# An exp queue's costs in an ordering simulation: two constants and the settings of an attention kernel's instruction order

## The chip, the cores and the metric

One core of a Trainium2 chip. The metric is the device time of one execution in microseconds; the median of three runs stands for a kernel.

## The reference

Attention with normalised queries and keys, 32 heads, 2048 positions, 20 columns per head, bf16 inputs:

```
qn = q / (sqrt(sum(q*q)) + 1e-6);  kn = k / (sqrt(sum(k*k)) + 1e-6)
logits = einsum('bhqd,bhkd->bhqk', qn, kn) * t[head]
out = einsum('bhqk,bhkd->bhqd', softmax(logits), v)
```

With 20 columns per head the matrix products are thin; the 32 x 2048 x 2048 exponentials are the bulk of the work.

## The kernel before

**Units.** Four heads form a group (eight groups), and 512 query positions of a group form a superblock (32 of them, `sb`). A superblock's scores fall into 64 units: one head, 128 key positions on the partitions, 512 queries along the columns; 2048 units in all. TensorE makes the scores of a unit with one matmul over a strip of 32 rows (line 793); four heads can run side by side on the four strips.

**Two ways to an exponential.** ScalarE takes two units at once: a *wave*, two matmuls into one of two slots of the PSUM tensor psA and one exp over 128 x 1024 into pA (line 995). VectorE takes single units: scores into a bank of psD, then one instruction that multiplies, adds and converts to int16, so that the bits read as float16 approximate an exponential (dI, line 361). GpSimd (POOL) adds two constants to these bits, as 64-bit integers of four values each, giving dS1 and dS2 (line 374); one POOL instruction can cover up to four units. Their weighted sum is the approximation.

**The second product.** A PV matmul (line 815) multiplies exponentials with v and a column of ones and accumulates in one bank of psD; the four heads of a round run side by side on four column strips. A unit from ScalarE needs one PV matmul (source pA), one from VectorE four (dI with vaug, dI with vhalf, dS1 and dS2 with vaug). At the end of a superblock VectorE transposes the bank out (accT, line 386), takes the reciprocal of the ones' column and multiplies (lines 400 and 401), and the output goes out by DMA.

**Preparation.** For each next group q, k and v are loaded on SP's queue, squares are summed (a transpose on SP, then small matmuls, line 749), the norms are worked out on VectorE, and q and k go through DMA transposes (line 446) to qT and kT. Early in the kernel, where TensorE has little to do, it runs matmuls on zeros (line 612), which the program calls heating.

**What sets the order.** `make_plan` simulates the five engines in steps of 5 ns while the program is built. Each operation has a `cost` (how long its engine is taken) and a `lat` (when its result is there); the engines choose by rules what to do next, and the order that comes out is each engine's instruction stream, with semaphore waits for the dependences. Which units go to ScalarE and which to VectorE also comes out of it: whoever is free first takes the next. An exp enters with these two values:

```
a = Op("ACT", "exp", ..., ACT0 + n_u * QW / 1200.0, ACT1 + n_u * QW / 1200.0)
```

For a wave n_u * QW is 1024. A psA slot is free for the next wave when the exp's `lat` is over, and the rules ask how far away that is: for instance, no PV round begins within PVHOLD of it. The rules' settings (`RULES`) can differ for every ten waves: character i of ORDER picks an entry of CHOICES, 23 sets of changed settings, for waves 10 i to 10 i + 9. On the chip only the order and the waits remain; each engine goes through its stream as fast as its waits allow.

The program holds a second plan, in which ScalarE makes all exponentials; a flag read from t picks one of the two at run time. In the runs here the first is used.

Of the kernel before, what the change touches and what calls it, by code (L numbers as in the profile page):

```python
# [30 lines left out]
CHOICES = ({}, dict(JOINB=1), dict(DURG=2), dict(RUN=2), dict(PVHOLD=(0, 0)), dict(PVHOLD=(.4, .4)), dict(DFIRST=0), dict(PVHOLD=(.33, .33)),  # L31
           dict(PRIO=1.1), dict(PMIN=3), dict(PGAP=.15), dict(JOINB=9), dict(TWICED=1), dict(PVHOLD=(.15, .15)), dict(POOL_MAX=2), dict(DURG=0),
           dict(PVHOLD=(.2, .3)), dict(PVHOLD=(.3, .2)), dict(NEEDW=1), dict(PSLACK=.1), dict(JOINB=1, DURG=2), dict(PVHOLD=(.2, .2), DURG=2), dict(BACK=12))
ORDER = "0305080i2k7lj3700hj2e0me07cj08i7a1i0j01g2bjb5j5080i00g017fl67g60"

PARTS = ((0, 4), (4, 16))
NH = 4
# [31 lines left out]
PV_MAX = 100  # L69
POOL0 = .162  # L70
POOLL = .05
ACT0 = .05
LOAD0 = 2.75
TRL = 2.25
TRK = 1.2
PLAG = .03
LOCKL = 0.12
ACT1 = .33
PEL = .17
POOL1 = .0009  # L80
POOL2 = .00166
# [75 lines left out]
def bass_standalone__qk_norm__prompt_kernel(  # L157
# [15 lines left out]
    with ExitStack() as es:  # L173
# [295 lines left out]
        def make_plan(share):  # L469
# [476 lines left out]
            def step_pe0():  # L946
# [25 lines left out]
                if parts and slot_free and not any(x[3] in held for x in pending_pv):  # L972
# [4 lines left out]
                    if keys_ready(us):  # L977
# [6 lines left out]
                        if cur > 0 and not cur_free() and in_use() < S.HEATQ:  # L984
# [11 lines left out]
                               [("psA", slot)], [("pA", pslot, i) for i in range(WAVES[slot])],  # L996
                               ACT0 + n_u * QW / 1200.0, ACT1 + n_u * QW / 1200.0)
                        P.link(a)
# [294 lines left out]
            while True:  # L1293
                if share and len(waves) // STRETCH > stretch:
                    stretch = len(waves) // STRETCH
                    vars(S).update(RULES, **CHOICES[int(ORDER[stretch:stretch + 1] or "0", 36)])
                moved = True
# [190 lines left out]
```

## Time and profile before

| | before |
|---|---|
| median of three runs | 596.71 us (596.52 to 599.08) |
| the profiled execution's own time | 596.55 us |
| its span, first to last instruction | 594.4 us |
| busy: TensorE, VectorE, ScalarE, POOL | 582.6, 574.4, 582.3, 498.2 us |
| mean granted TensorE clock | 0.998 |
| exps on ScalarE | 630 |

Busy time is the union of an engine's records. A record of ScalarE or VectorE can overlap the next on its engine, and matmuls are pipelined, so a busy engine is not necessarily one that could do no more: the distance between the ends of records tells more than their lengths. "PE" is TensorE's matmul, "PEld" its weight load, "SPq" the issue of a DMA. In the tables a row has the source line, engine, operation, and result<-sources.

### The profile page before, as it was taken

To read this page: it belongs to the slowest core of one execution; us is meant where nothing else is said; L and a number is where in the kernel's file an instruction comes from. 1 tells how busy PE (TensorE), PEld (TensorE's weight loads), DVE (VectorE), ACT (ScalarE), POOL (GpSimd) and SP (SyncE) were. 2 spreads that over 40 slices of the span, in tenths; PEclk is the share of its full clock that TensorE was granted. 3 is DMA by queue.
4 is the path that set the end of the run, shared out by engine and by line. 5 is a ranking of instruction groups with operands and counts; after the bars stand their busy time and mean duration, and the time that the engine had idled before them with its cause. 6 is when DMAs were issued, how large, how long until landed. Compare 5 with 4: busy or idle time off the path is not lost.

```text
span 594.4 us, 16322 instructions
## 1 busy us (share of the span) xinstructions
PE 582.6 (98%) x6741; PEld 154.0 (26%) x6741; DVE 574.4 (97%) x1012; ACT 582.3 (98%) x638; POOL 498.2 (84%) x947
## 2 busy tenths in 40 slices
PE   8999999999999999999999999999999999999996
PEld 4332222322222222222222222222222222222221
DVE  6899999999999999999999999999999999999995
ACT  6999999999999999999999999999999999999995
POOL 2498898888988879879898889978899798999995
PEclk9999999999999999999999999999999999999999
DMA  8701405105042051410534022340405204010000
GB/s 117 107 2 26 92 2 67 25 1 116 3 45 46 2 116 8 62 23 3 113 22 72 2 52 67 24 68 2 99 2 52 57 1 73 2 24 8 1 13 10
DMA packets 132143, 24.18 MB, mean 41 GB/s; under 512 B 121312, under 2 KB 132064, under 8 KB 132064
## 3 DMA queue, kind: packets, MB, share of 16 engines
q1 hardware_dynamic: 131264, 22.96, 24.4%
q8 instruction: 54, 0.88, 0.7%
q14 instruction: 25, 0.20, 0.1%
q10 hardware_dynamic: 800, 0.12, 0.1%
HBM read 7.87 MB, written 2.62 MB: 18 GB/s over the span
## 4 chain that ended last, share of the span: by engine, by line
ACT 83%; PE 13%; SPq 1%; POOL 1%; DMA 1%; DVE 1%; issue 0%
ACT pA L995 83%; PE psD L815 7%; PE psA L793 5%; POOL dS L374 1%; PE psD L612 1%; SPq L437 1%; DMA vaug<-in_v_dram 1%; PE psD L793 1%; DVE dI L361 0%; SPq L427 0%; DVE accT L386 0%; DVE ost L401 0%; SPq L577 0%; PE psD L658 0%; DVE rec L400 0%
## 5 line engine op out<-in xcount | busy, mean ns | idle before, releaser
L995 ACT ACTIVATE pA<-psA 128x1024 f16<-128x1024 f32 (+1 forms) x630 | 578.1, 1254 | 1.8 <-PE psD L793 0.9
L374 POOL INT64_ADD dS<-dI x931 | 491.8, 544 | 77.6 <-DVE dI L361 14.6
L361 DVE TENSOR_SCALAR dI<-psD 128x512 int16<-128x512 f32 (+1 forms) x764 | 488.1, 695 | 8.1 <-PE psD L793 5.6
L793 PE MATMUL psA<-qT,kT 32*128 32x512 bf16 x1260 | 245.2, 384 | 2.2 <-ACT pA L995 0.8
L793 PE MATMUL psD<-qT,kT 32*128 32x512 bf16 x793 | 240.7, 383 | 0.1
L815 PE MATMUL psD<-dS,vaug 128*22 128x512 f16 x1576 | 196.3, 383 | 1.4 <-POOL dS L374 1.4
L815 PE MATMUL psD<-pA,vaug 128*22 128x512 f16 (+1 forms) x1260 | 172.5, 383 | 1.1 <-DMA vaug<-in_v_dram 0.9
L815 PE MATMUL psD<-dI,vaug 128*22 128x512 f16 x788 | 130.6, 382 | 0.0
L815 PE MATMUL psD<-dI,vhalf 128*22 128x512 f16 x788 | 128.6, 383 | 0.0
L793 PEld LDWEIGHTS psA<-qT,kT 32*128 32x128 bf16 x1260 | 59.1, 91 | 251.7 <-ACT pA L995 246.2
L793 PEld LDWEIGHTS psD<-qT,kT 32*128 32x128 bf16 x793 | 56.3, 91 | 7.4 <-issue 3.6
L815 PEld LDWEIGHTS psD<-dS,vaug 128*22 128x22 bf16 x1576 | 42.1, 89 | 57.4 <-issue 30.7
L815 PEld LDWEIGHTS psD<-pA,vaug 128*22 128x22 bf16 x1260 | 36.7, 89 | 49.3 <-issue 45.4
L815 PEld LDWEIGHTS psD<-dI,vhalf 128*22 128x22 bf16 x788 | 28.2, 89 | 30.9 <-issue 21.7
L815 PEld LDWEIGHTS psD<-dI,vaug 128*22 128x22 bf16 x788 | 29.0, 89 | 23.1 <-issue 17.6
L386 DVE STREAM_TRANSPOSE accT<-psD 128x512 f32<-128x512 f32 x32 | 22.6, 705 | 2.7 <-PE psD L815 2.7
L401 DVE TENSOR_TENSOR ost<-accT,rec 128x320 bf16<-128x320 f32 x32 | 16.4, 512 | 0.1
L264 DVE TENSOR_TENSOR sqs<-qk 128x1280 bf16<-128x1280 bf16 x14 | 11.9, 849 | 0.0
L749 PE MATMUL psD<-ind,sqT 128*128 128x128 bf16 x140 | 11.6, 221 | 0.0
L749 PEld LDWEIGHTS psD<-ind,sqT 128*128 128x128 bf16 x140 | 7.9, 98 | 5.2 <-issue 5.0
L612 PE MATMUL psD<-zt 128*128 128x128 bf16 x106 | 9.2, 221 | 0.0
L322 DVE RECIPROCAL rn<-rsa 128x128 f32<-128x128 f32 (+2 forms) x10 | 7.8, 780 | 0.1
(59 smaller groups left out, 81.5 us busy)
## 6 DMA issues: line engine op xcount, KB each, us to landing
vaug<-in_v_dram SPq DMA_DIRECT2D x32, 80.0 KB, 4.2
qk<-in_k_dram SPq DMA_DIRECT2D x7, 320.0 KB, 4.4
out_dram<-ost SPq DMA_DIRECT2D x28, 80.0 KB, 1.9
qk<-in_q_dram SPq DMA_DIRECT2D x6, 320.0 KB, 4.1
qk<-in_q_dram SPq DMA_DIRECT2D x4, 80.0 KB, 2.8
out_dram<-ost SPq DMA_DIRECT2D x7, 40.0 KB, 2.0
qk<-in_k_dram SPq DMA_DIRECT2D x1, 240.0 KB, 3.6
qk<-in_q_dram SPq DMA_DIRECT2D x1, 240.0 KB, 4.3
```

The lines of the kernel that those rows point to most:

```text
L264: ops.append(dve("sq", w_, R2, lambda e, o=sq, x=x3: e.tensor_tensor(o, x, x, ALU.mult), [("qk", b, a, i) for i in parts] + [("qkx", b, i) ...
L322: add("inv", lambda e: e.reciprocal(rn_, ra), [K("ra")], RN[a0:a1], R1, n * 5 * R1)
L361: lambda e: e.tensor_scalar(dst, psD[:, pb * QW:(pb + n) * QW], 1024.0 * LOG2E, 15360.0 - 1024.0 * LOG2K + SHIFTS[0], ALU.mult, ALU.add),
L374: lambda e: e.int64_add(o.bitcast(U64), x.bitcast(U64), add), rd, wr)
L386: return dve("drain", QW, R1, lambda e: e.transpose(accT[:, 16 * b:16 * b + 16, :].rearrange("p b d -> p (b d)"), psO_(sb)), [("psD", OB(s ...
L401: dve("omul", 320 * n, R1, lambda e: e.tensor_tensor(dst, num, rcb, ALU.mult), at + ar, [("ost", hg % 2, g) for g in range(g0, g1)]),
L437: ops.append(dma("ldv", lambda e, d=d_, s=s_: e.dma_start(d, s), [], [("v", b, hh)], 1.4, 4.0))
L612: return lambda e: e.matmul(bank, zt[:, 0:128], zt[:, 0:n], start=False, stop=False, skip_group_check=True)
L749: mms = [lambda e, g=g, j=j: e.matmul(dst, sqT[:, (5 * g + j) * 128:(5 * g + j + 1) * 128], ind[:, j, 96 - 32 * g:224 - 32 * g], start=g + ...
L793: return lambda e: e.matmul(dst, lhsT, rhs, tile_position=(32 * hh, 0))
L815: return lambda e: e.matmul(dst, lhsT, rhs, start=first, stop=last, skip_group_check=True, tile_position=(0, 32 * hh))
L995: a = Op("ACT", "exp", lambda e, s=src, d=dst: e.activation(d, s, ACT.Exp), [("psA", slot)], [("pA", pslot, i) for i in range(WAVES[slot]) ...
```

## The change

Two costs of an exp in the simulation, and the string of settings:

```
-ORDER = "0305080i2k7lj3700hj2e0me07cj08i7a1i0j01g2bjb5j5080i00g017fl67g60"
+ORDER = "01i6e8h7238em08g57h5hi2i0gi1j2i0lgea8aa50a567i6538abh965h237050"
...
-ACT0 = .05
+ACT0 = .0633
...
-ACT1 = .33
+ACT1 = .17
```

For a wave the simulated distance between two exps on ScalarE goes from 0.903 to 0.917 us, and the time from an exp's start to its result from 1.183 to 1.023 us. No instruction's form changes. The order does, on all engines. In the streams of the two built programs, first plan:

| | before | after |
|---|---|---|
| exps (waves) | 630 | 628 |
| units for VectorE | 788 | 792 |
| dI instructions (of them double) | 764 (24) | 768 (24) |
| int64 adds on POOL | 931 | 935 |
| PV matmuls | 4412 | 4424 |
| heating matmuls | 106 | 123 |
| PV phases of one, two, three rounds | 141, 434, 29 | 153, 387, 55 |
| PV matmuls behind the last psA pair | 28 | 40 |

A phase is a run of PV matmuls between two other operations of TensorE.

## The prediction

> **What bounds the kernel now.** I read the page's busy shares first, then the chain that ended last, then the windows of the middle, to see whether the engine named by the chain ever rests.
>
> ```profile
> span 594.4 us, 16322 instructions
> PE 582.6 (98%) x6741; PEld 154.0 (26%) x6741; DVE 574.4 (97%) x1012; ACT 582.3 (98%) x638; POOL 498.2 (84%) x947
> ACT 83%; PE 13%; SPq 1%; POOL 1%; DMA 1%; DVE 1%; issue 0%
> ```
>
> Three engines look full, so shares decide nothing. The chain says ScalarE, and its pieces in order of time (start, length, what) say where:
>
> ```profile
> 25.59 6.11 POOL dS L374 x14
> 31.75 0.40 PE psD L815 x4
> 32.47 0.80 PE psD L815 x12
> 33.62 491.45 ACT pA L995 x536
> ...
> 587.09 1.69 PE psD L815 x28
> 588.80 0.73 DVE accT L386
> ```
>
> One unbroken piece of 536 exps takes 491.45 us: 0.9169 us for each wave of 1024 columns. Behind 525 us the chain hops between engines, but the windows show ScalarE busy to the last hundredth there too (columns: length, then busy time and count of PE, PEld, DVE, ACT, POOL, then clock, DMA share, GB/s):
>
> ```profile
> 40.00:140.00 100.00, 99.83 (x1149) 25.15 (x1146) 99.06 (x169) 100.00 (x111) 84.69 (x161) 1.00 0.25 42
> ...
> 540.00:580.00 40.00, 39.89 (x484) 10.32 (x480) 38.97 (x68) 40.00 (x45) 38.02 (x73) 1.00 0.04 8
> sum 540.00, PE 538.32 PEld 136.55 DVE 534.87 ACT 540.00 POOL 470.28; mean PE 89.72 PEld 22.76 DVE 89.14 ACT 90.00 POOL 78.38
> ```
>
> ACT 540.00 of 540.00: from 40 us on the kernel is a queue of exps at 0.917 us. So I ask of the change: how many exps, can they start to be dense sooner, does anything let the queue run dry, and what follows the last one.
>
> **How much lateness the queue forgives.** An exp's record is longer when it queues behind the one before it:
>
> ```profile
> L995 ACT ACTIVATE pA<-psA x630: 1018/1262/1346, 8.6 to 587.1; 128x1024 f16<-128x1024 f32 x157, 128x1024 bf16<-128x1024 f32 x1
> ```
>
> (minimum/median/maximum in ns.) 1.02 us is an exp that found the engine free, 1.346 one whose scores came as early as two psA slots allow. TensorE may thus be up to 1.346 - 1.018 = 0.33 us late with a wave before ScalarE idles. This stretch of TensorE shows how it gets late:
>
> ```profile
> 134.62 0.39 PE L793 MATMUL psA<-qT,kT 32*128 32x512 bf16 x2
> ...
> 135.69 0.39 PE L793 MATMUL psA<-qT,kT 32*128 32x512 bf16 x2
> 135.70 0.60 PE L793 MATMUL psD<-qT,kT 32*128 32x512 bf16 x2
> 136.23 0.60 PE L815 MATMUL psD<-dS,vaug 128*22 128x512 f16 x6
> ...
> 136.77 0.39 PE L793 MATMUL psA<-qT,kT 32*128 32x512 bf16 x2
> 136.78 0.39 PE L793 MATMUL psD<-qT,kT 32*128 32x512 bf16 x1
> 137.09 0.60 PE L815 MATMUL psD<-pA,vaug 128*22 128x512 f16 x5
> ...
> 137.64 0.39 PE L793 MATMUL psA<-qT,kT 32*128 32x512 bf16 x2
> ```
>
> From one psA pair to the next: 1.07 us with three rounds of four PV matmuls behind it, 1.08 with two score passes and two rounds (both scores of a strip in one phase), 0.87 with one pass and two rounds. The first two are long against 0.917, by 0.16 each; the ordinary one wins 0.046 back. The exps of that place:
>
> ```profile
> L995 ACT ACTIVATE pA<-psA x3: 1023/1027/1187, 136.1 to 138.1; 128x1024 f16<-128x1024 f32 x3
> ```
>
> Two long stretches on end, 0.33 in sum, use up all the allowance (1.023) and still cost nothing. That is the scale by which I judge the new order.
>
> **The change, part by part.** All counts are of the two built programs' instruction orders. The two constants and the settings act only through the order, so its effects are these.
>
> *Fewer waves.* 630 exps become 628; four units of work go to VectorE instead (792 for 788). ScalarE: 2 x 0.917 = 1.83 us less on the path. A rule that would make this term vanish: by the Trainium skill's page Perfetto Trace Analysis (section Optimizing Scalar/DVE Operations) an instruction of ScalarE on PSUM costs about 51 ns beside its elements, an estimated 0.904 us for such a wave, which is the old setting's pitch; the trace's 0.917 over 536 waves disagrees and decides.
>
> *More on VectorE.* Four more dI instructions (768 for 764, 24 of them double in both). The first eight show their pitch:
>
> ```profile
> 22.90 4.93 DVE L361 TENSOR_SCALAR dI<-psD 128x512 int16<-128x512 f32 x8 [0.88 <-PE psD L793]
> L361 DVE TENSOR_SCALAR dI<-psD 128x512 int16<-128x512 f32 x740 | 461.1, 678 | 7.7 <-PE psD L793 5.5 <-PE psA L793 0.3
> ```
>
> (4.93 - 0.68)/7 = 0.61 us, so +2.4 us. Its window also shrinks: by the 1.83, by the start term below, and by another 1.83 because the last unit for VectorE now stands in the fifth wave from the end instead of the third: some 5 us. Against 7.3 us in all stand 5.1 us of visible idle in the windows (540 - 534.87), and bubbles inside busy time: 461.1/740 = 0.623 where 0.61 is the pitch, about 10 us over 740. It fits, with little left. I put it at 0 and keep 4 us as the upper end. POOL gets four more int64 instructions (935 for 931) and has 70 us idle in the windows. On SP nothing is added; in one head group q's transpose goes ahead of k's, in others four output transfers swap with a transpose. Each group has some 74 us (594/8), so I take 0; without that cover a landing is at stake:
>
> ```profile
> kT<-kpad SPq DMA_TRANSPOSE x8, 4.3
> ```
>
> *TensorE's order.* The mean work between two waves, from passes, rounds and switches as above, is the same, 0.878 us in both orders. But it is spread less evenly: long stretches (over 0.95) go from 54 to 87 behind the 28th wave, PV phases of three rounds from 29 to 55. I added up lateness along both orders (stretch minus 0.917, never below 0). Before: highest 0.34 and 0.34, at the place shown and at one near 470 us; the trace has exps of 1.02 us at exactly these. After: highest 0.37 in one cluster around wave 484, then 0.33 and 0.30. Against 0.33 that is an idle of some 0.05 us. I allow 0.2 for this and for waits on POOL that fall badly; lower end 0, since a queue that is never dry cannot gain.
>
> *The start.* Here the queue does run dry:
>
> ```profile
> 22.99 4.75 ACT L995 ACTIVATE pA<-psA 128x1024 f16<-128x1024 f32 x5
> 25.59 1.89 POOL L374 INT64_ADD dS<-dI  x5 [7.38 <-DVE dI L361]
> 27.90 0.10 PEld L815 LDWEIGHTS psD<-dS,vaug 128*22 128x22 bf16 x4 [1.73 <-POOL dS L374]
> 28.66 5.98 ACT L995 ACTIVATE pA<-psA 128x1024 f16<-128x1024 f32 x6 [0.92 <-PE psD L793]
> ```
>
> The exps end at 27.74, the next at 28.66 + 1.02 = 29.68: 1.94 for 0.917, 1.03 lost. The sixth of that piece ends at 34.64 (28.66 + 5.98) where 29.68 + 5 x 0.917 = 34.27 would do: 0.37 lost. Cause: the first int64 add runs at 25.59, though its input was there near 23.6 (22.90 + 0.68); it waits for something that no row names; I take it to be the cost of POOL's first instruction of this kind. The first PV on dS waits for the sixth POOL instruction. In the new order the same PV stands one wave later (+0.917 us), and waits for the fifth, since the first ones take two units at once. At 1.89/5 = 0.38 each that is 25.59 + 5 x 0.38 = 27.5, against an arrival of TensorE near 27.2: 0.3 us late instead of 1.43, inside the allowance. So 1.40 us go, if POOL starts at 25.59 again. Ends: 0 to 1.40; I take 1.40, because both facts (a wave later, one POOL instruction fewer) point the same way. Seventeen more heating matmuls (123 for 106) lie ahead of this, where TensorE waits for ScalarE; uncovered, each would cost
>
> ```profile
> 20.13 0.68 PE L612 MATMUL psD<-zt 128*128 128x128 bf16 x9
> ```
>
> (0.68 - 0.23)/8 = 0.06 us, 1 us in all.
>
> *The tail.* Behind the last psA pair stood 28 PV matmuls, now 40.
>
> ```profile
> 583.36 4.96 ACT L995 ACTIVATE pA<-psA 128x1024 f16<-128x1024 f32 x5
> 586.70 0.39 PE L793 MATMUL psA<-qT,kT 32*128 32x512 bf16 x2
> 587.02 0.40 PE L815 MATMUL psD<-pA,vaug 128*22 128x512 f16 x4
> ```
>
> ScalarE ends at 588.32, TensorE 0.47 later (588.79). A round is (1.69 - 0.40)/6 = 0.215, so three more are 0.65. Before, the last pair was 0.16 late behind a three-round stretch; after, only two-round ones stand ahead of it, and it should come about 0.24 earlier against the exps. Net +0.41; ends 0 and +0.65.
>
> **The sum.** -1.83 - 1.40 + 0.41 + 0.2 = -2.6. The profiled execution took 596.55 us (594.4 of span, 2.15 around it), so 593.9; the median of the runs is 596.71, 0.16 above, so I say 594.1 for the median. A measurement of this kernel can tell about 0.5%, 3.0 us, from no change: 593.7 is the border of faster, and the forecast lies just inside "same".
>
> **The rivals.**
>
> *The start's stall stays* or moves to the next PV that needs POOL: -1.83 + 0.41 = -1.4, 595.3. For it: POOL's late start isn't touched by the change. Against: the later PV.
>
> *VectorE runs out of slack.* ScalarE then waits for scores whose bank VectorE hasn't freed. Against: the bubbles above. Price: up to the 4 us that I couldn't cover, 595 to 598.
>
> *The long stretches bite* (the other side). The new costs let TensorE be late by design; if the allowance in practice is below 0.16 us, because waits on POOL already use half of it, each long stretch empties the queue by 0.16. The 33 more alone: 5.3 us, 599.4; all 87: 14 us, 608. I take 601. Against it speaks the place at 136 us; for it that the wait table has 136 waits for POOL:
>
> ```profile
> PEld psD L815 <- POOL dS L374: 38.5, 136, 1.7
> ```
>
> (38.5 us in sum, the longest 1.7.) It decides from a lateness of 0.33 on.
>
> *ScalarE isn't the limit*: its own pitch is smaller, and TensorE paces it. Then two waves fewer bring nothing, and start and tail leave -1.0: 595.7. The mechanism would show as exps of 1.02 us throughout; the median is 1262. This is where the 51 ns of the Trainium skill (Perfetto Trace Analysis) would lead.
>
> *More than summed*: the tail hides its rounds and nothing is late: -1.83 - 1.40 = -3.2, 593.5.
>
> **How the numbers follow.** Forecast 0.53 (its own range 593.4 to 594.9), start stays 0.14, VectorE 0.13, long stretches 0.14, ScalarE not the limit 0.03, more than summed 0.03. Faster by over 0.5% (under 593.7): about 0.4 of the forecast's own case, and the last: 0.25. Slower by over 0.5% (over 599.7): most of the long stretches, a little of VectorE: 0.14. Same: 0.61. For 8 in 10 I leave out the long stretches and trifles below: 593.1 to 598.6.
>
> **What would show it.** Right: 628 exps; one ScalarE piece of the chain at 0.917 per wave; the last exp ending near 585.1 (588.32 - 3.23) and the last transpose of accT starting near 586.0; TensorE's wait for dS near 27.5 us under 0.5. The start is wrong if ScalarE still has a gap of 0.9 near 28 us; the queue step is wrong if the windows from 40 us on show ACT under 100.00, and the partner named in ScalarE's waits (a dI bank or a dS) tells VectorE from the long stretches. The forecast as a whole is wrong above 595.

## The result: 594.4 us for 596.5

The changed kernel takes 594.38 us (median of 9 runs, 593.94 to 594.82), the kernel before 596.52 (median of 9); the ratio is 0.9961, 95% interval 0.9949 to 0.9974: 2.1 us or 0.4% less, clear of noise but inside "same" (under 0.5%), and 0.3 from the forecast of 594.1. As a change it is -2.1 where -2.6 was forecast: the median of the kernel before is 596.52 in this group of runs, 0.2 below the 596.71 that the forecast started from. The profiled execution took 594.49 us. Its page:

```profile
span 592.7 us, 16383 instructions
PE 581.3 (98%) x6768; PEld 160.2 (27%) x6768; DVE 574.6 (97%) x1016; ACT 580.4 (98%) x636; POOL 500.9 (84%) x951
ACT 87%; PE 10%; DVE 2%; POOL 1%; issue 0%
L995 ACT ACTIVATE pA<-psA 128x1024 f16<-128x1024 f32 (+1 forms) x628 | 576.2, 1201 | 0.5 <-PE psD L793 0.2
```

The shares say nothing new. The count does (628), and so does the mean of an exp: 1201 ns where it was 1254. The line before was

```profile
L995 ACT ACTIVATE pA<-psA 128x1024 f16<-128x1024 f32 (+1 forms) x630 | 578.1, 1254 | 1.8 <-PE psD L793 0.9
```

The exps queue less long, TensorE is later with them. The chain in order of time:

```profile
25.35 3.87 POOL dS L374 x8
...
51.27 517.24 ACT pA L995 x564
...
584.58 2.30 PE psD L815 x40
586.90 0.73 DVE accT L386
```

ScalarE's piece has 517.24/564 = 0.9171 us per wave, against 0.9169 before: still dense, with 0.2 us of idle time hidden in it (564 x 0.9167 = 517.02). The start, from ScalarE's, POOL's and TensorE's rows in order of time:

```profile
9.47 20.34 ACT L995 ACTIVATE pA<-psA 128x1024 bf16<-128x1024 f32 x22 [0.19 <-PE psA L793]
25.35 2.69 POOL L374 INT64_ADD dS<-dI  x6 [6.93 <-DVE dI L361]
27.72 0.10 PEld L815 LDWEIGHTS psD<-dS,vaug 128*22 128x22 bf16 x4 [0.42 <-POOL dS L374]
29.27 0.10 PEld L815 LDWEIGHTS psD<-pA,vaug 128*22 128x22 bf16 x3 [0.59 <-POOL dS L374]
30.03 8.36 ACT L995 ACTIVATE pA<-psA 128x1024 f16<-128x1024 f32 x9 [0.22 <-PE psD L793]
```

The first PV on dS runs at 27.72 instead of 27.90 although POOL starts almost as late (25.35 for 25.59); one wave later in the order, it costs ScalarE nothing. A later PV round that waits for POOL (29.27, for 0.59 us) does: the 22nd exp ends at 9.47 + 20.34 = 29.81, and the next one at 30.03 + 1.02 = 31.05, 1.24 behind for 0.917. So 0.33 us are lost, where the kernel before lost 1.40 in this part.

Added up from the ends of all exp records (distances above 0.917), up to the last transpose of accT, in us:

| | before | after | difference |
|---|---|---|---|
| waves x 0.917 | 630 | 628 | -1.83 |
| first exp's end, with the wait for v behind the first waves | 10.32 | 10.54 | +0.22 |
| ScalarE idle, 20 to 40 us | 1.39 | 0.33 | -1.06 |
| ScalarE idle behind 40 us | 0.00 | 0.32 | +0.32 |
| last exp's end to the last transpose of accT | 0.49 | 0.93 | +0.44 |
| sum | | | -1.91 |
| start of that transpose, measured | 588.80 | 586.90 | -1.90 |

The second row isn't the order's: over the fourteen profiles of this study it lies between 10.0 and 10.7, as the loads land. The third row is one execution's, too: before_exp6 and before_qk33 (below), whose first 40 us are those of the kernel before, lost 1.10 and 1.02 there, and after_exp6 and after_dve8 0.22 and 0.24. So the start's gain is 0.7 to 1.2 us.

The table ends at the last transpose of accT, and two stretches lie outside it. From that transpose to the end of the span it is 5.58 us before and 5.84 after (5.5 to 6.4 over the fourteen profiles). And an execution's time exceeds its span by 2.17 us before and 1.75 after: by 2.1 to 2.3 in the runs of the kernel before, by 1.7 to 1.9 in those of the changed one. For the two profiled executions -1.90 + 0.26 - 0.42 = -2.06, from 596.55 to 594.49. What makes the 0.42 no run here shows.

### The profile page after: what moved, and what is told of

It reads as the page before. It is cut to its first block, busy times and chain, and to the rows that moved or that the text cites. A ratio compares the mean times of both kernels' runs of the same rounds, so it can differ in the third digit from the quotient of the medians.

```text
span 592.7 us, 16383 instructions
## 1 busy us (share of the span) xinstructions
PE 581.3 (98%) x6768; PEld 160.2 (27%) x6768; DVE 574.6 (97%) x1016; ACT 580.4 (98%) x636; POOL 500.9 (84%) x951
## 4 chain that ended last, share of the span: by engine, by line
ACT 87%; PE 10%; DVE 2%; POOL 1%; issue 0%
ACT pA L995 87%; PE psD L815 4%; PE psA L793 3%; PE psA L616 1%; PE psD L612 1%; POOL dS L374 1%; DVE dI L361 0%; PE psD L793 0%; PE psD L749 0%; DVE ssum L294 0%; DVE accT L386 0%; DVE sqs L291 0%; DVE kpad L338 0%; PE psD L616 0%; DVE ost L401 0%
## 5 line engine op out<-in xcount | busy, mean ns | idle before, releaser
L995 ACT ACTIVATE pA<-psA 128x1024 f16<-128x1024 f32 (+1 forms) x628 | 576.2, 1201 | 0.5 <-PE psD L793 0.2
L793 PE MATMUL psD<-qT,kT 32*128 32x512 bf16 x795 | 237.6, 383 | 0.1
L815 PE MATMUL psD<-dS,vaug 128*22 128x512 f16 x1584 | 201.2, 383 | 0.1
L815 PE MATMUL psD<-pA,vaug 128*22 128x512 f16 (+1 forms) x1256 | 181.1, 383 | 0.3 <-POOL dS L374 0.3
L815 PE MATMUL psD<-dI,vaug 128*22 128x512 f16 x792 | 133.9, 383 | 0.0
L815 PE MATMUL psD<-dI,vhalf 128*22 128x512 f16 x792 | 131.4, 383 | 0.0
L815 PEld LDWEIGHTS psD<-pA,vaug 128*22 128x22 bf16 x1256 | 39.6, 89 | 49.6 <-issue 41.2
L815 PEld LDWEIGHTS psD<-dI,vhalf 128*22 128x22 bf16 x792 | 29.7, 89 | 27.4 <-issue 20.0
L612 PEld LDWEIGHTS psD<-zt 128*128 128x128 bf16 x123 | 7.0, 98 | 4.9 <-issue 4.9
```

Of the source, the lines that this page charges most:

```text
L612: return lambda e: e.matmul(bank, zt[:, 0:128], zt[:, 0:n], start=False, stop=False, skip_group_check=True)
L793: return lambda e: e.matmul(dst, lhsT, rhs, tile_position=(32 * hh, 0))
L815: return lambda e: e.matmul(dst, lhsT, rhs, start=first, stop=last, skip_group_check=True, tile_position=(0, 32 * hh))
L995: a = Op("ACT", "exp", lambda e, s=src, d=dst: e.activation(d, s, ACT.Exp), [("psA", slot)], [("pA", pslot, i) for i in range(WAVES[slot]) ...
```

## The experiments

Each prediction of a kernel stands on the sum that the forecast used: waves, idle time at the start, lateness over 0.33 us, tail. The medians are compared with the kernel before in the same group of runs.

**One half of the change each.** The costs without the settings, the settings without the costs, and both without the new latency:

```
costs_only:  ACT0 = .0633, ACT1 = .17, ORDER as before
order_only:  ACT0 = .05,   ACT1 = .33, ORDER as after
pitch_only:  ACT0 = .0633, ACT1 = .33, ORDER as after
```

> The two new costs with the old settings. The order that comes out has 632 waves (before 630, after 628), 81 long stretches of TensorE, 52 PV matmuls behind the last psA pair, and the first PV on dS at the old place behind six POOL instructions. Theory (ScalarE is a dense queue; time is waves x 0.917 + losses at the start + tail): +1.83 for the waves, the start's 1.4 us stay, six more rounds in the tail +1.1; 599.4 against 596.5, 598.8 to 600. Rival (long stretches empty the queue, 0.16 each): 27 more of them add 4.3 us, 603.7.

> The new settings with the two old costs. The order has 632 waves, 86 long stretches, 88 PV matmuls behind the last psA pair, and the first PV on dS one wave later behind five POOL instructions. Theory: +1.83 for the waves, -1.1 to -1.4 at the start, +3.0 for fifteen more rounds in the tail, some 0.3 of lateness over 0.33: 600.1 against 596.5, 599.4 to 600.8. Rival (long stretches): +5.1 on top, 605.

> The new settings and the new distance of 0.917 with the old latency of 1.183. The order has 628 waves like the changed kernel, 68 PV matmuls behind the last psA pair and 107 long stretches. Theory: the waves' gain is the distance's alone; +1.5 for seven more rounds in the tail than the changed kernel has, +1.1 of lateness over 0.33 by adding up the order: 597.0 against 594.4 for the changed kernel and 596.4 before. Rival (the latency is what counts): 599 or more.

Measured: costs_only 599.21 for 596.35 (ratio 1.0045, 1.0031 to 1.0058); order_only 600.81 for 596.35 (1.0072, 1.0059 to 1.0086); pitch_only 597.72 for 596.47 (1.0016, 1.0003 to 1.0028). Expected were 599.4, 600.1 and 597.0: the first was met, the second came out at the upper end of its range, the third 0.7 above. All three are slower than the kernel before, so here the gain needs both halves. With the old latency alone (pitch_only) the order has the same 628 waves as the changed kernel and takes 3.3 us more. The ends of their chains (costs_only, order_only, pitch_only):

```profile
588.13 2.94 PE psD L815 x51
591.10 0.73 DVE accT L386
```

```profile
588.49 4.89 PE psD L815 x88
593.40 0.73 DVE accT L386
```

```profile
586.24 3.81 PE psD L815 x68
590.07 0.73 DVE accT L386
```

With the last exps ending at 589.41, 589.88 and 587.47 the tails are 1.7, 3.5 and 2.6 us for 52, 88 and 68 PV matmuls; the kernel before has 0.5 for 28. Their long stretches (81, 86, 107) cost 0.2, 0.7 and 2.0 us of idle time behind 40 us, where adding up lateness had given some 0.3 for the second and 1.1 for the third. So a long stretch has no fixed price, and for these two the sum was too kind by about a factor of two. The rival of 0.16 each is out (603.7, 605). The 3.3 us of pitch_only over the changed kernel are 1.7 in the tail and 1.7 of idle time behind 40 us.

**ScalarE longer by six exps.** The added exp reads the same scores and writes to a tile of its own:

```
+ again = [id(o) for o in plans[0][0].order["ACT"] if o.name == "exp"][90::90][:6]
+ again = {x: again_scr for x in again}
...
+ elif id(o) in again:
+     o.emit(eng, d=again[id(o)][:, :])
+     o.emit(eng).then_inc(sems[e], 1)
```

> The kernel before with six of its exps done twice, the first time into a tile of its own (waves 90, 180, ... 540); the order is untouched. Theory (ScalarE is the limit from the first waves to the end): 6 x 0.917 = +5.5 us, 602.0 against 596.5. Rival (ScalarE is paced by TensorE): 0 to 1.

> The changed kernel with six exps done twice in the same way. Theory (still ScalarE): +5.5 less what little idle time there is behind the first 40 us, 599.9 against 594.4, 599.4 at least. Rival (VectorE or TensorE has become the limit in stretches): clearly less than 5.5, say 2 to 4, since an exp more would fall into waiting time.

Measured: 601.67 for 596.66 (1.0073, 1.0052 to 1.0095) and 599.98 (1.0041, 1.0017 to 1.0066, against the kernel before; the changed kernel stands at 0.9961). Two pieces of the second one's chain:

```profile
92.98 82.50 ACT pA L996 x90
176.40 82.55 ACT pA L996 x90
```

92.98 + 82.50 = 175.48, the next piece begins at 176.40: the exp between them costs its whole 0.92. Within a piece 82.50/90 = 0.9167. In the changed kernel ScalarE is still the limit, with 0.05 of idle time in some pieces.

**VectorE and TensorE longer.** In the changed kernel eight dI instructions are done twice; in the kernel before 33 waves have their score matmuls done twice:

```
+ again = [... order["DVE"] if o.name == "P1" and o.cost < .7][85::85][:8]      (after_dve8)
+ again = set(... order["PE"] if o.name == "QKA"][40::17][:33])                  (before_qk33)
+ for mm in o.info * (1 + (id(o) in again)):
```

> The changed kernel with eight of VectorE's dI instructions done twice, the first time into a tile of its own, 85 apart; the order is untouched. Theory (VectorE's bubbles can close): at most 8 x (0.61 - 0.33) = 2.2 us where TensorE is late by more than the allowance, more likely 0 to 1: 594.4 to 595.4. Rival (VectorE has no slack left): 8 x 0.61 = 4.9 us, 599.3.

> The kernel before with the score matmuls of 33 waves done twice (every 17th from wave 40), 0.21 us more for TensorE at each; 80 long stretches instead of 54. Theory (lateness up to 0.33 us is forgiven): adding lateness up along the order leaves 0.4 us over the allowance, 596.9 against 596.5. Rival (a long stretch costs ScalarE 0.16): +5.3, 601.8.

after_dve8: 596.45 (0.9993 against the kernel before, 0.9971 to 1.0016), 2.0 us over the changed kernel: the upper end of what the theory allowed (8 x (0.61 - 0.33) = 2.2), not the 4.9 of a VectorE that is full. Its exp records give 2.35 us of idle time behind 40 us for 0.32: 0.25 more for each added instruction on average, of the 0.61 that it takes, and between 0.14 and 0.33 in the 8 us behind each. TensorE's waits for a dI bank (sum, number, longest), in the changed kernel and in this one:

```profile
PEld psD L793 <- DVE dI L361: 4.8, 22, 0.4
PEld psD L794 <- DVE dI L362: 8.7, 33, 0.5
```

Eleven waits more: VectorE's delay reaches ScalarE through TensorE's queue, and on average 0.36 us of it are forgiven, about the 0.33 of the theory. "More likely 0 to 1" was too hopeful.

before_qk33: 597.37 for 596.66 (1.0003, 0.9975 to 1.0031); the runs of this group scatter more than the effect. The traced execution took 596.53, one of the shorter ones, so the trace tells what the added matmuls cost in it and not what made others longer. Its exps (minimum/median/maximum) and ScalarE's piece of the chain:

```profile
L995 ACT ACTIVATE pA<-psA x630: 1017/1162/1322, 9.2 to 587.1; 128x1024 f16<-128x1024 f32 x157, 128x1024 bf16<-128x1024 f32 x1
33.22 491.81 ACT pA L995 x536
```

491.81 for 536 waves, 0.36 more than before (491.45), the median exp 1162 for 1262: 33 delays of 0.21 us are eaten by the queue almost whole, as added up (0.4). The +5.3 of the rival is out by the times as well.

**POOL's first add.** One more int64 add, on zeros, early in POOL's stream:

```
+ o = Op("POOL", "warm", lambda e: e.int64_add(wscr[...], zt[...], 0), ["zt", ...], ["wscr"], 0.01, 0.05)
```

> The kernel before, with one more int64 add on POOL, on zeros into a tile of its own, ahead of POOL's last early memsets; every other instruction stands as it was. Theory: what delays POOL's first real add until 25.6 us is the cost of its first instruction of that kind; paid some 2 us earlier, the adds begin near 23.7 us, the 1.4 us of ScalarE's idle time near 28 to 34 us go: 595.1 against 596.5. Rival (the adds wait for something else): no change, 596.5.

> The changed kernel with the same early int64 add. Theory: its remaining idle time of ScalarE near 30 us (0.33) goes, 594.1 against 594.4; the later PV on dS of the new order has taken the rest already. Rival (the new order's start owes nothing to POOL): 594.4.

Measured: 596.10 for 596.35 (0.9998, 0.9989 to 1.0007) and 594.54 (0.9964). By the times next to nothing changed, as if the cause were wrong. POOL's rows of before_warm say otherwise:

```profile
16.06 0.74 POOL L536 MEMSET kpad<- 128x768 bf16 x1 [4.20 <-DVE sqs L292]
22.70 0.20 POOL L609 INT64_ADD wscr<-zt  x1 [5.90 <-issue]
22.86 0.73 POOL L536 MEMSET qpad<- 128x768 bf16 x1
23.53 0.81 POOL L536 MEMSET vaug<- 128x64 bf16 x2
25.25 1.15 POOL L375 INT64_ADD dS<-dI  x3 [0.90 <-DVE dI L362]
```

The 5.9 us of idle time moved ahead of the added instruction, so they are the cost of the first one. But three memsets and the run-time branch between the two plans now stand behind them (the memsets end at 24.34, the branch is recorded at 25.08), and the first real add comes at 25.25 again. The 0.90 that its row puts down to VectorE is the branch's: the dI it needs was there near 23.65. The next pair puts the added instruction ahead of all memsets:

> The kernel before with the early int64 add again, now ahead of all four early memsets on POOL, so that neither they nor the branch stand behind its 6 us; all other instructions as they were. Theory (POOL's first int64 add costs some 6 us once, and this made the first PV on dS late): the first real add runs near 23.7 us, the 1.0 to 1.4 us of ScalarE's idle time near 28 to 34 us shrink to 0.2: 595.4 against 596.4. Rival (something else holds the adds until 25.2): no change.

> The changed kernel with the early int64 add ahead of the memsets. Theory: the new order's adds wait for VectorE almost as long as for POOL, so of its 0.33 us near 30 us only a part goes, 0 to 0.3: 594.2 against 594.4. Rival: as much as in the kernel before, 1 us, 593.4.

```profile
17.96 0.20 POOL L610 INT64_ADD wscr<-zt  x1 [5.98 <-issue]
...
23.97 2.34 POOL L375 INT64_ADD dS<-dI  x6 [3.68 <-DVE dI L362]
```

Measured: before_warm2 595.41 for 596.47 (0.9982, 0.9972 to 0.9992), 1.1 us less, and 0.20 us of idle time at the start for 1.02 to 1.39. Not all of the 1.1 is the start's: the median span is 0.7 shorter (593.6 for 594.3), and the time outside the span 0.35 shorter, as in the changed kernel. after_warm2 594.47 (0.9961, 0.9947 to 0.9975): nothing measurable beyond the changed kernel; in its trace 0.10 for 0.33.

**The tail.** The last six settings changed by a search for a shorter tail, on top of after_warm2:

```
-ORDER = "...h965h237050"
+ORDER = "...h965h20d8bd"
```

> after_warm2 with the last six settings changed (20d8bd for 237050): TensorE's order is the same up to wave 596, there are still 628 waves, and 28 PV matmuls instead of 40 stand behind the last psA pair. Theory: the last exp ends where it did, the last transpose starts 0.48 behind it instead of 0.93; 0.45 less than after_warm2, 593.8. Rival (the tail was hidden, or the new last waves come late): no change against after_warm2.

Measured: 593.24 (0.9944, 0.9926 to 0.9961), the fastest of all kernels here, 1.2 us under after_warm2 and 3.2 under the kernel before. ScalarE's piece and the last transpose:

```profile
10.57 549.32 ACT pA L1000 x599
...
586.04 0.73 DVE accT L387
```

The last exp ends at 585.55, so the tail is 0.48 as expected. 599 waves take 549.32, 0.9171 each, from the second wave on: the start's losses are gone as well. But 0.45 less than after_warm2 was expected, and 1.2 less came. In the two traces the last transpose starts 0.39 earlier (586.43 and 586.04), and the stretch behind it, which the expectation had taken as fixed, is 0.93 shorter (6.43 and 5.50). Why is open.

All kernels side by side, in us; idle time and tail from the exp records of one execution each, the sum against the kernel before (630 waves, 1.39, 0.00, 0.49), the last column by medians against the kernel before in the same group of runs. An added exp counts as a wave:

| kernel | waves | idle 20 to 40 us | idle later | tail | sum | measured |
|---|---|---|---|---|---|---|
| after | 628 | 0.33 | 0.32 | 0.93 | -2.1 | -2.1 |
| costs_only | 632 | 0.56 | 0.20 | 1.68 | +2.4 | +2.9 |
| order_only | 632 | 0.45 | 0.72 | 3.52 | +4.6 | +4.5 |
| pitch_only | 628 | 0.48 | 2.04 | 2.60 | +1.4 | +1.3 |
| before_warm2 | 630 | 0.20 | 0.00 | 0.48 | -1.2 | -1.1 |
| after_warm2 | 628 | 0.10 | 0.17 | 0.94 | -2.5 | -2.0 |
| after_tail_warm | 628 | 0.00 | 0.13 | 0.48 | -3.1 | -3.2 |
| before_warm | 630 | 0.98 | 0.00 | 0.48 | -0.4 | -0.3 |
| after_warm | 628 | 0.38 | 0.32 | 0.94 | -2.1 | -1.8 |
| before_exp6 | 636 | 1.10 | 0.00 | 0.48 | +5.2 | +5.0 |
| after_exp6 | 634 | 0.22 | 0.36 | 0.93 | +3.3 | +3.3 |
| after_dve8 | 628 | 0.24 | 2.35 | 0.93 | -0.2 | -0.2 |
| before_qk33 | 630 | 1.02 | 0.42 | 0.48 | 0.0 | +0.7 |

Four terms give every kernel but before_qk33 within 0.5 us. That is a little better than they deserve, since the first exp's end, the stretch behind the last transpose and the time outside the span, which they leave out, move by up to 0.6, 1.0 and 0.5 us from kernel to kernel and in part cancel.

## Why the prediction was right, step by step

**The sum.** The four terms were forecast at -2.6 and measured at -2.1, each with the right sign: -1.83, -1.06 for -1.40, +0.32 for +0.2, +0.44 for +0.41. That the time came out within 0.3 us is partly luck. The signs named for the path were missed by 0.9: the last exp ends at 585.97 for 585.1, the last transpose starts at 586.90 for 586.0. The start lost 0.34 more than forecast, the first exps came 0.22 later, and the 0.32 of lateness had been left out of these two signs. Outside the span, where the forecast kept its 2.15 us without a reason, 0.42 went the other way.

**The bound.** Right: ScalarE's queue of 0.917 us per wave, shown by the six added exps in both kernels. **Fewer waves.** -1.83, as forecast; what yields 628 is the new distance together with the new settings (pitch_only has 628 with the old latency; costs_only and order_only, with one of the two, have 632).

**The start.** The mechanism held, the size was too large: -1.40 forecast, -1.06 measured (0.7 to 1.2 over the other traces). The sum priced one PV and one rate of POOL. An add over two units takes longer here:

```profile
25.35 1.20 POOL L374 INT64_ADD dS<-dI  x2 [6.93 <-DVE dI L361]
```

That is 0.60 each, not the 0.38 of the single ones. For the first PV this did no harm: it ran at 27.72 with a wait of 0.42, near the 27.5 and 0.3 forecast. But the PV round at 29.27 waited 0.59 us for POOL's eighth add, one of 0.81 us (28.40 to 29.21). What failed is that the step said "inside the allowance" for the first PV and stopped there. The cause of POOL's late start, which I only argued, is shown by before_warm2. The Trainium skill states it: GPSIMD Engine Reference, section 2.1 Instruction dispatch, puts the first call of freshly loaded code at about 6 us without a record of its own; the traces agree (5.90 and 5.98).

**Lateness.** 0.2 allowed, 0.32 measured, in four places. The cluster forecast around wave 484 is there; its exps:

```profile
L995 ACT ACTIVATE pA<-psA x6: 1018/1024/1117, 453.6 to 458.4; 128x1024 f16<-128x1024 f32 x6
```

Half of these six are at the floor of about 1.02, and 0.08 us is lost. The largest loss, 0.15 near 52 us, was not in my count:

```profile
50.62 0.38 PE L793 MATMUL psA<-qT,kT 32*128 32x512 bf16 x1
50.63 0.38 PE L793 MATMUL psD<-qT,kT 32*128 32x512 bf16 x1
50.85 0.37 PE L793 MATMUL psA<-qT,kT 32*128 32x512 bf16 x1
```

A psD matmul stands between the two halves of the wave, and the second half runs 0.23 later than the first; the exp starts at 51.26, when the second is done. (That the two share a strip of rows is my reading; the rows don't tell.) I had counted a wave from its first half.

**The tail.** +0.41 forecast, +0.44 measured. That the tail is on the path is shown by the trace of after_tail_warm: 0.46 less tail, the last transpose 0.39 earlier. **VectorE.** Put at 0; no run isolates the four more instructions, but the sum closes without them, and after_dve8 shows the price when a delay doesn't fit: 0.25 us each on average, not 0.61. The rival "VectorE runs out of slack" is out at this load, "long stretches bite" at its price.

**Where the reading was weaker than it looked.** "ACT 540.00 of 540.00" was taken as proof that the queue is never dry. After the change the same sum reads

```profile
sum 540.00, PE 536.95 PEld 141.91 DVE 537.07 ACT 539.95 POOL 476.53; mean PE 89.49 PEld 23.65 DVE 89.51 ACT 89.99 POOL 79.42
```

0.05 of rest, where the ends of the exps show 0.32 of lost time: a record of 1.02 us covers the next 0.10 us of an engine that could have ended another exp after 0.917. By the sign named for it (ACT under 100.00 in the windows from 40 us on) the queue step would count as wrong; the loss is 0.32 us of 540, so it was mis-sized by 0.1 and not wrong. For the kernel before the conclusion was true, but the length of the chain's piece over its count carried it, not the busy share.

## What to carry to other kernels

Where one engine is a dense queue, a change of order is worth what it does to four numbers: how many items the queue has, what it loses before it is dense, by how much its feeder's lateness exceeds what the queue forgives, and what stands behind its last item. All four can be read or estimated before a run, the first and the last best (from the instruction order and the measured 0.215 us of a round), the lateness worst (1.1 for 2.0 in pitch_only). Settings and the costs of the simulation act together: either half of this change alone was slower than neither. One pair of orders doesn't make this a rule.

## What the hardware showed that was not expected

The first int64 add on POOL cost 5.90 and 5.98 us in the two places where it was put, and the rows of POOL show it only as idle time. Put ahead of three memsets and the branch it did little, since these then waited behind it; put into an idle stretch of the engine before them it took 0.8 to 1.2 us from ScalarE's idle time (before_warm2). And an exp of 1024 columns has three lengths: 1.02 us alone, up to 1.35 as recorded in a full queue, and 0.917 from end to end, of which only the last one counts where the queue is dense.
